# Four heads' first decay sums by TensorE, slot tables three passes ahead, a first network layer 44 steps ahead

## The chip, the core and the metric

The kernel runs on one core of one Trainium2 chip. The metric is the device time of one execution in microseconds, as the median of several runs. Three runs of the kernel before gave 884.05, 885.95 and 887.55 us, so its median is 885.95 us.

## The reference

Three stages follow each other, all in float32.

1. Attention with decay: batch 4, 8 heads, 576 positions, head size 64. The scores are `q·k/8`, plus `min(-(cum[i] - cum[j]), 0)`, where `cum` is the running sum of `max(s, 0)` along a head, under a causal mask; then softmax, then the product with `v`.
2. A mixture of experts over the 2304 rows of 512 numbers that attention leaves. Each row goes to the one expert (of 8) with the largest gate logit: `gate * relu(x @ w1[e]) @ w2[e]`, hidden size 1024.
3. A dense network: `h = x @ w_in` (2048 wide), `g = h * clip(h + 3, 0, 6) / 6`, `out = g @ w_out`.

The outputs are 2304 x 512 float32 numbers.

## The kernel before, in words

Products of float32 numbers are made of float16 halves: each operand is split into a high and a low half, and three products (high-high, high-low, low-high) stand for one. The splitting is done by ScalarE (high half) and VectorE or GpSimd (low half).

**Attention** runs over 20 units (a batch and a chunk of 128 rows, the last chunk 64), four pairs of heads to a unit. For a pair n, one turn of the main loop (from line 997 on) issues the transposes of pair n-1, the scores of pair n+1 (`S`, line 554), the addition of the decay sums with the row minimum on VectorE (`A`, line 567), the exponential on ScalarE (`E`, line 573), the split of the transposed weights (`CD`, lines 603 and 604), and the products with `v` of pair n-2 (`V`, line 637). `A` needs the decay sums of its head copied to all 128 partitions. These are made once: `s` is clipped and scaled (line 394), summed by one VectorE scan over 576 columns for the 32 rows of batch and head (line 395), put into an interleaved order of rows by ScalarE (lines 397 and 401), stored to DRAM as `cum_d` (line 403), and read back with one row copied to 128 partitions (`load_cum`, line 410) into the tile `cp`. For batch 0 the first 256 columns come first, in two loads: heads 0 and 1, then heads 2 to 7. Behind these, in the same queue of SyncE (SP), stand the loads of `v` for two row chunks, of `k` and `q` of the next 256 rows, and the five loads of the gate weights.

**The experts** run as 10 passes of 224, 224, 128, 128, 360, 336, 320, 296, 288 and 272 rows (numbers 0 to 9). The row numbers of a pass are a small table, `slots`, which SP loads from DRAM (`load_slots`, line 197). With it GpSimd gathers the rows (`gather`, line 204, up to three blocks of 128 rows by 2 KB), and SP transposes them by DMA into the tile `xsT` (`turn`, line 215). There are two buffers of `xsT`, one for even passes and one for odd ones. In pass p the rows of pass p+2 are gathered. Before the change the slots of pass p+2 are loaded in pass p too, just ahead of that gather (lines 1198 to 1201), for p from 3 on; those of passes 2 to 4 are loaded during pass 0. In pass p from 4 on, the weights of pass p+1 come in eight loads `wf` of 512 KB (line 239) through five staging buffers, and two or three pieces of `w_in` (`wd`, line 1049) through the same five; ScalarE and VectorE split them (lines 254 and 257, and 1037 to 1060). The first product of a pass is line 1109 (`ph`), whose result is turned into halves on ScalarE and VectorE (`hT`, lines 1113 and 1114); the second product is line 1221 (`py`).

**The network** has 9 chunks of 256 rows and 8 steps to a chunk, 72 steps in all. A first-layer step (`hidden_step`) is 24 matmuls (line 1247) into one PSUM bank; the bank is then clipped by ScalarE and VectorE (lines 1254 and 1255) and stored to DRAM (`t_d`). A second-layer step (`out_products`, line 1330) is 21 matmuls, three into each of seven banks in the order 6, 5, 4, 1, 0, 2, 3; what it needs is fetched back from `t_d` (`fetch`, lines 1307 to 1309) and combined (`sum_step`, lines 1318 to 1320, 1258 and 1259). The first `AHEAD` hidden steps use the seven banks in turn (step modulo 7); later ones use bank 7 alone. AHEAD is 40, so 41 hidden steps run before the first second-layer step, and after that one hidden step is made for two second-layer steps. During the first 41 steps, after every fifth, `convert` splits one of eight pieces of `w_out`, some 8 us of VectorE work each; it is tied behind the newest clip on VectorE.

**What sets the order.** Each engine works through its own queue in order, and so does SP with its DMA issues. The order in a queue is set when the program is built: the framework walks the instructions in the order of the program text, with modelled durations, and puts on each engine what is ready by that model. `issue_after` adds a fixed order on one engine. `at_slot(n, f)` calls f at the end of turn n of the attention loop.

Of the kernel before, what the change touches and what calls it, by code (L numbers as in the profile page):

```python
# [8 lines left out]
F32 = mybir.dt.float32  # L9
# [3 lines left out]
AF = mybir.ActivationFunctionType  # L13
ALU = mybir.AluOpType
# [21 lines left out]
def kernel(  # L36
# [16 lines left out]
    nc = tc.nc  # L53
    B, H, S, D = q.shape
# [10 lines left out]
    SC = 8.0  # L65
# [28 lines left out]
    idf = cst.tile([128, 128], F32, name="idf")  # L94
# [7 lines left out]
        out=upper, in_=upper, pattern=[[1, 128]], base=-1, channel_multiplier=-1,  # L102
# [47 lines left out]
    PF = 2 * NS  # L150
    rank_of = lambda p: NE - NS + p - NS if p < PF else p - PF
    NPASS = len(passes)
# [42 lines left out]
    def load_slots(p):  # L195
        n = (passes[p] + 127) // 128
        nc.sync.dma_start(slots[:, p, :n], rows_of(p, 128 * n).rearrange("(x q) o -> q x o", q=128))
# [24 lines left out]
    stage, mark = {}, {}  # L222
    rt = ctx.enter_context(tc.tile_pool(name="rt", bufs=2))
    psT = ctx.enter_context(tc.tile_pool(name="psT", bufs=3, space=PSUM))
# [79 lines left out]
    with ExitStack() as at:  # L304
        ac = at.enter_context(tc.tile_pool(name="ac", bufs=1))
        a2 = at.enter_context(tc.tile_pool(name="a2", bufs=2))
# [5 lines left out]
        kTs, cums, loaded, qTs, both = {}, {}, {}, {}, {}  # L312
# [34 lines left out]
        BH = B * H  # L347
        s_sb = a2.tile([BH, S], F32, tag="ne", name="s_sb")
# [20 lines left out]
        for o in (0, 64):  # L369
# [4 lines left out]
            for r in range(2):  # L374
                nc.gpsimd.affine_select(
                    out=mk[rows, r], in_=mk[rows, r], pattern=[[-1, 64]], base=0, channel_multiplier=1,
# [13 lines left out]
        zero = a2.tile([BH, S], F32, tag="ne", name="zero")  # L390
        nc.vector.memset(zero, 0.0)
        run = a2.tile([BH, S], F32, tag="pp", name="run")
        cum_sb = a2.tile([BH, S], F32, tag="pp", name="cum_sb")
        nc.vector.tensor_scalar(out=s_sb, in0=s_sb, scalar1=0.0, scalar2=SC, op0=ALU.max, op1=ALU.mult)
        nc.vector.tensor_tensor_scan(out=run, data0=s_sb, data1=zero, initial=0.0, op0=ALU.add, op1=ALU.add)
        nf = S // 128 * 128
        nc.scalar.activation(
            cum_sb[:, :nf].rearrange("h (j r p) -> h j p r", r=2, p=64),
# [6 lines left out]
        def load_cum(b, hs, a=0, z=S):  # L405

            if b not in cums:
                cums[b] = a2.tile([128, H, S], F32, tag="cp", name="cp")
            rows = cum_d.rearrange("(b h o) t -> b o h t", b=B, o=1)[b, :, hs, a:z]
            return nc.sync.dma_start(cums[b][:, hs, a:z], rows.partition_broadcast(128)[:, 0])  # L410

        def fold_cum(b, p):

# [437 lines left out]
        def at_slot(n, f):  # L851
            todo.setdefault(n, []).append(f)
# [21 lines left out]
        def then(f, *args):  # L874
            with tc.issue_after(last[0]):
                last[0] = f(*args).ins

        some, rest = slice(0, 2), slice(2, H)
        then(load_cum, 0, some, 0, 256)
        then(load_cum, 0, rest, 0, 256)  # L880
        then(load_v, 0, 0)
        then(load, 0, 1)
        then(load_v, 0, 1)
# [3 lines left out]
        then(load_v, 0, 2)  # L887
        then(load_v, 0, 3)
        then(load, 0, 2)
        for x, fs in enumerate(prep(0, 0, fast=True)):  # L890
            for f in fs:
                f() if x < 2 else at_slot(x - 3, f)
# [173 lines left out]
    HO = KO // 2  # L1066
# [60 lines left out]
    with ExitStack() as ex_:  # L1127
# [6 lines left out]
        jobs, pend = [], []  # L1134
        DOUBLES = {4: 3, 5: 3, 6: 3, 7: 2, 8: 2, 9: 3}
        for p, rows in enumerate(passes):
# [5 lines left out]
            if fresh:  # L1142
# [3 lines left out]
                jobs = new + jobs  # L1146
# [33 lines left out]
            for f in range(KF):  # L1180
# [10 lines left out]
                if p and f % 2 == 1:  # L1191

                    a, z = (min(sum(passes[:x]), NT) for x in (p, p + 1))
# [1 line left out]
                        with after("act"):  # L1195
                            nc.gpsimd.memset(x2T[:, f // 2::KD, a:z], 0.0)
                feed(f)
            if p >= PF - 1 and p + 2 < NPASS:
                load_slots(p + 2)
            if p and p + 2 < NPASS:  # L1200
                got = gather(p + 2)
                if p != NS:
# [13 lines left out]
            for d in range(KD):  # L1216
                py = pb.tile([128, 512], F32, tag="p", name="py")
                cols = slice(128 * d, 128 * d + 128)
                for f in range(KF):
                    for x, (i_, j_) in enumerate(((0, 0), (0, 1), (1, 0))):  # L1220
                        nc.tensor.matmul(  # L1221
                            py[:, :rows], wt2[:, j_, f, cols], hT[i_][:, f, :rows],
                            start=(f == 0 and x == 0), stop=(f == KF - 1 and x == 2),
# [43 lines left out]
    with ExitStack() as mx_:  # L1267
# [15 lines left out]
        jobs = [pair_piece(c, lambda c=c: w_sums[c]) for c in range(HO)]  # L1283
        pend = []
        TC = 256
        NSTEP = NT // TC * HO
        AHEAD = NSTEP - (NSTEP - HO) // 2
        t_d = dram.tile([NSTEP, 128, 512], F32, name="t_d")
        banks = [psT.tile([128, 512], F32, tag="T", name="bank") for x in range(3)]
        banks += [pb.tile([128, 512], F32, tag="p", name="bank") for x in range(5)]  # L1290
# [1 line left out]
        def hidden_step(s):  # L1292
            c, f = divmod(s, HO)
            x2 = x2T[:, :, TC * c:TC * c + TC]
            ph = banks[s % 7 if s < AHEAD else 7]
            for x, f_ in enumerate((f, f + HO)):
# [5 lines left out]
        def fetch(s):  # L1302


            if s < NSTEP:
                t = t_d[s].rearrange("p (a n) -> p a n", n=128)
                nc.sync.dma_start(back[s % 4][:, 0:2], t[:, 1:3])
                nc.sync.dma_start(back[s % 4][:, 2:4], t[:, 0::3])
                nc.sync.dma_start(back[s % 4][:, 4], t[:, 0])

        def sum_step(s):


            if s >= NSTEP:
                return
            vtt = nc.vector.tensor_tensor
            t, hi, lo = back[s % 4], sets[:, s % 4, 0], sets[:, s % 4, 1]
            vtt(out=t[:, 5:7], in0=t[:, 0:2], in1=t[:, 2:4], op=ALU.subtract)
            vtt(out=t[:, 7:9], in0=t[:, 0:2], in1=t[:, 3:5], op=ALU.add)
            vtt(out=t[:, 9], in0=t[:, 2], in1=t[:, 3], op=ALU.add)  # L1320
            halves_of(hi, lo, t[:, 3:10])
# [42 lines left out]
        def convert():  # L1364
            while jobs and len(pend) < 2:
                pend.append(jobs.pop(0)())
            if pend:
                with tc.issue_after(mark["clip"]):
                    pend.pop(0)()

        done = 0
        for l in range(NSTEP - 4):
            upto = min(NSTEP, AHEAD + l // 2 + 1)
            while done < upto:
                hidden_step(done)
                done += 1
                if done == 6:
                    nc.sync.dma_start(orows, row_d[:NT].rearrange("(c p) o -> p c o", p=128)[:, :, 2])
                if l == 0 and done % 5 == 1:
                    convert()  # L1380
                if done in (28, 30, 32, 34):
                    fetch((done - 28) // 2)
                if done in (37, 39):
                    sum_step((done - 37) // 2)
            fetch(l + 4)
            sum_step(l + 2)
            out_products(l)
            if l % HO == HO - 1:
                out_rows(l // HO)
# [8 lines left out]
    with ExitStack() as fb:  # L1398
# [5 lines left out]
        stop = nc.values_load(nblk, min_val=0, max_val=NT // 128)  # L1404
        with tc.For_i(0, stop, 1):
# [5 lines left out]
                out=t8, in0=iota8[:, None, 0].to_broadcast(of_all), in1=expert[:, :, None].to_broadcast(of_all), op=ALU.is_equal  # L1411
            )
            V.tensor_tensor(out=t8, in0=t8, in1=limit[:, None].to_broadcast(of_all), op=ALU.mult)
            rest, mine = f1.tile([128, NU], F32, name="rest"), f1.tile([128, NU], F32, name="mine")
# [6 lines left out]
            for x, m in enumerate((ones, upper)):  # L1421
# [3 lines left out]
                out=mine[:, 1:], data0=pn[:, 0, :NU - 1], data1=mine[:, 1:], initial=0.0, op0=ALU.add, op1=ALU.add  # L1425
# [13 lines left out]
            for u in range(NU):  # L1439
                n = R[units[u][1]]  # L1440
                nc.gpsimd.indirect_dma_start(
                    out=again_d[:, :], out_offset=Offset(ap=to[:n, u:u + 1], axis=0),
# [6 lines left out]
                out=xw, out_offset=None, in_=x_d[:, :], in_offset=Offset(ap=at[:, 0:1], axis=0)  # L1449
# [8 lines left out]
                out=sel, in0=iota8[:, 0], scalar1=ge[:, 3:4], scalar2=ge[:, 1:2],  # L1458
                op0=ALU.is_equal, op1=ALU.mult,
# [16 lines left out]
            for f in range(KO):  # L1476
# [11 lines left out]
                out=out[:, :], out_offset=Offset(ap=at[:, 2:3], axis=0), in_=o, in_offset=None,  # L1488
# [32 lines left out]
```

## Time and profile before

| | us |
|---|---|
| median of three runs | 885.95 |
| the profiled execution | 887.8 |
| its span in the profile | 886.1 |
| TensorE (PE) busy | 801.7 |
| VectorE (DVE) busy | 623.7 |
| ScalarE (ACT) busy | 461.8 |
| GpSimd (POOL) busy | 295.0 |

The profiled execution took 887.8 us, of which 886.1 us lie in the span that the trace covers. Attention fills the span up to about 290 us, the expert passes run from about 276 to 510 us, and the network from there to 874 us. In the rows, "L567" is line 567 of the kernel; a group reads "output<-inputs"; what stands in square brackets is the idle time of that engine just before, and what ended it. SPq is the DMA-issuing queue of SyncE. A matmul's duration includes its way through the array, so in a stream of matmuls the count in a stretch tells more than the durations.

### The profile page before, as it was taken

The numbers are of one execution on the slowest core, as the hardware profiler recorded it, in microseconds if no ns is written. First come the engines' busy times: TensorE is split into PE (matmuls) and PEld (weight loads), VectorE is DVE, ScalarE is ACT, GpSimd is POOL, SyncE is SP. The second block draws the span as 40 slices with busy tenths as digits, with TensorE's granted clock in tenths as the row PEclk, the third lists the DMA queues.
The fourth block names the chain that finished last, engine by engine and source line by source line (L and its number), as shares of the span: only waits on it lengthen the run. The fifth ranks groups of instructions, "written<-read, shape, count | busy, mean of one in ns | idle before, by whom it ended". The sixth has DMA issues, their size and how long they took to land. (4 is left out here: it accounts for less than half of the span.)

```text
span 886.1 us, 21854 instructions
## 1 busy us (share of the span) xinstructions
PE 801.7 (90%) x8332; PEld 661.9 (75%) x8332; DVE 623.7 (70%) x1545; ACT 461.8 (52%) x853; POOL 295.0 (33%) x397
## 2 busy tenths in 40 slices
PE   5898888779778989899998999999899999999993
PEld 3677666666558987566776888888788888888883
DVE  4787876766576653877787679878677677767770
ACT  3787776777854342665555444554334433343440
POOL 2585856689862222132430200000022022211222
PEclk9999999998789999999999999999999999999997
DMA  7966345333425486987879346544344444444430
GB/s 175 269 145 191 86 101 167 59 106 100 144 56 141 126 216 181 284 297 226 238 235 331 107 141 203 213 164 150 126 150 148 127 155 151 151 132 151 153 101 27
DMA packets 154327, 142.30 MB, mean 161 GB/s; under 512 B 68710, under 2 KB 122214, under 8 KB 153446
## 3 DMA queue, kind: packets, MB, share of 16 engines
q1 hardware_dynamic: 150422, 130.76, 49.9%
q0 software_dynamic: 3792, 10.06, 3.7%
q8 instruction: 67, 1.10, 0.5%
q14 instruction: 46, 0.38, 0.2%
HBM read 106.97 MB, written 28.54 MB: 153 GB/s over the span
## 5 line engine op out<-in xcount | busy, mean ns | idle before, releaser
L1247 PE MATMUL bank<-x2T,wi 128*128 128x256 f16 x1728 | 194.2, 273 | 0.6 <-POOL x2T L1229 0.5
L1247 PEld LDWEIGHTS <-wi 128*128 128x128 f16 x1728 | 169.1, 98 | 20.5 <-issue 1.0
L1330 PE MATMUL bank<-wo,sets 128*128 128x256 f16 x1512 | 172.7, 274 | 4.9 <-DVE cl L1255 4.0
L1330 PEld LDWEIGHTS <-sets 128*128 128x128 f16 x1512 | 148.5, 98 | 23.8 <-issue 4.4
L1221 PE MATMUL py<-hT,t 128*128 128x224 f16 (+7 forms) x960 | 111.0, 276 | 8.1 <-DVE hT L1114 6.7
L1258 ACT ACTIVATE sets<-back 128x896 f16<-128x896 f32 x72 | 68.2, 950 | 94.1 <-PE bank L1330 77.1
L1109 PE MATMUL ph<-xsT,t 128*128 128x224 f16 (+7 forms) x960 | 109.9, 276 | 7.3 <-DVE hT L1114 7.3
L1221 PEld LDWEIGHTS <-t 128*128 128x128 f16 x960 | 86.7, 99 | 31.2 <-issue 10.9
L1341 POOL TENSOR_TENSOR u<-sa 128x256 f32<-128x256 f32 x9 | 9.5, 1054 | 301.1 <-ACT sa L1340 301.1
L1109 PEld LDWEIGHTS <-t 128*128 128x128 f16 x960 | 86.2, 99 | 28.3 <-issue 8.0
L1259 DVE SCALAR_TENSOR_TENSOR sets<-back,sets 128x896 f16<-128x896 f32 x72 | 80.2, 1119 | 32.7 <-ACT sets L1258 32.6
L604 DVE SCALAR_TENSOR_TENSOR lo<-pt,hi 128x256 f16<-128x256 f32 (+3 forms) x144 | 72.7, 519 | 30.8 <-ACT hi L603 30.5
L257 DVE SCALAR_TENSOR_TENSOR t<-wf,t 128x1024 f16<-128x1024 f32 x53 | 64.5, 1221 | 36.6 <-ACT t L254 36.4
L582 PE MATMUL pt<-idf,pp 128*128 128x128 f32 (+1 forms) x400 | 77.1, 307 | 9.4 <-DVE den L649 3.6
L603 ACT ACTIVATE hi<-pt 128x256 f16<-128x256 f32 (+3 forms) x144 | 63.9, 461 | 41.4 <-PE pt L582 33.4
L254 ACT ACTIVATE t<-wf 128x1024 f16<-128x1024 f32 x53 | 55.6, 1055 | 45.0 <-DMA wf<-in_moe_w_dram 41.3
L573 ACT ACTIVATE pp<-ne,nm 128x128 f32<-128x128 f32 (+4 forms) x144 | 76.8, 580 | 4.3 <-DVE nm L567 4.1
L637 PE MATMUL o<-v,hi 128*128 128x65 f16 (+2 forms) x960 | 63.6, 203 | 14.6 <-ACT hi L603 7.8
L567 DVE CUSTOM_DVE_ANT_0 ne<-sp,cp 128x128 f32<-128x128 f32 (+4 forms) x144 | 61.1, 456 | 19.3 <-ACT pp L573 9.9
L637 PEld LDWEIGHTS <-hi 128*128 128x128 f16 (+2 forms) x960 | 49.0, 107 | 26.7 <-ACT hi L603 11.3
L582 PEld LDWEIGHTS pt<-idf,pp 128*128 128x128 f32 (+1 forms) x400 | 46.7, 151 | 19.2 <-remote 3.5
L637 PE MATMUL o<-v,lo 128*128 128x65 f16 (+2 forms) x480 | 54.2, 202 | 1.7 <-DVE lo L604 1.7
(202 smaller groups left out, 1231.5 us busy)
## 6 DMA issues: line engine op xcount, KB each, us to landing
wf<-in_moe_w_dram SPq DMA_DIRECT2D x64, 512.0 KB
back<-t_d SPq DMA_DIRECT2D x144, 128.0 KB
wd<-in_moe_w_in_dram SPq DMA_DIRECT2D x16, 512.0 KB
wd<-in_moe_w_out_dram SPq DMA_DIRECT2D x16, 512.0 KB
cp<-cum_d SPq DMA_DIRECT2D x6, 1152.0 KB
t_d<-cl SPq DMA_DIRECT2D x24, 256.0 KB
t_d<-sets SPq DMA_DIRECT2D x24, 256.0 KB
t_d<-wo SPq DMA_DIRECT2D x24, 256.0 KB
```

Of the source, the lines that this page charges most:

```text
L257: stt(out=lo, in0=fv, scalar=sc, in1=hi, op0=ALU.mult, op1=ALU.subtract)
L573: mark["act"] = nc.scalar.activation(self.view(self.pp, e), self.view(self.ne, e), AF.Exp, bias=self.nm[:, e:e + 1], scale=-1.0).ins
L582: nc.tensor.transpose(self.pt[g][:m, x, :], src, idf)
L603: nc.scalar.activation(hi, pt, AF.Copy, scale=SP)
L604: stt(out=lo, in0=pt, scalar=SP, in1=hi, op0=ALU.mult, op1=ALU.subtract)
L637: mark["pe"] = nc.tensor.matmul(dst, a, x, start=first, stop=last).ins
L1109: mark["pe"] = nc.tensor.matmul(ph[:, :n], wt[c][:, a, cols], xT[:, KD * b_ + c, :n], start=(c == 0 and x == 0), stop=(c == KD - 1 and x = ...
L1221: nc.tensor.matmul(py[:, :rows], wt2[:, j_, f, cols], hT[i_][:, f, :rows], start=(f == 0 and x == 0), stop=(f == KF - 1 and x == 2),)
L1247: m = nc.tensor.matmul(dst, wi[:, a, kk, fs], x2[:, KD * b_ + kk], start=(kk == 0 and x == 0), stop=(kk == KD - 1 and x == 2),)
L1258: nc.scalar.activation(hi, t, AF.Copy, scale=SG)
L1259: stt(out=lo, in0=t, scalar=SG, in1=hi, op0=ALU.mult, op1=ALU.subtract)
L1330: m = nc.tensor.matmul(banks[k_][:, :HM], sets[:, s % 4, a, k_], w_sums[f][:, b_, k_], start=(f == 0 and x == 0), stop=(f == HO - 1 and x ...
```

## The change

Four edits are made.

- The clip of `s` and the scan are each cut in two: columns 0 to 127 first, then 128 to 575, with the second scan starting from the last column of the first.
- `first_cum` makes the decay sums of heads 0 to 3 for the first 128 columns on TensorE: for each head a float32 product of a column of the identity (copied to 128 columns) with the 32 x 128 running sums, into one PSUM bank of the pool that the transposes use, and one ScalarE copy of 128 x 512 into `cp`. It is called at slot -1. The two loads from `cum_d` change: heads 4 to 7 of columns 0 to 255 first, then heads 0 to 3 of columns 128 to 255.
- The slots of pass p+3 are loaded in pass p, for p from 2 to 6.
- AHEAD becomes 44, so that 45 hidden steps run before the first second-layer step, and then 7 hidden steps are made for 16 second-layer steps. The first fetches and sums keep their distance to AHEAD. The first piece of `w_out` is no longer tied behind the newest clip.

```diff
-        nc.vector.tensor_scalar(out=s_sb, in0=s_sb, scalar1=0.0, scalar2=SC, op0=ALU.max, op1=ALU.mult)
-        nc.vector.tensor_tensor_scan(out=run, data0=s_sb, data1=zero, initial=0.0, op0=ALU.add, op1=ALU.add)
+        for a, z in ((0, 128), (128, S)):
+            nc.vector.tensor_scalar(out=s_sb[:, a:z], in0=s_sb[:, a:z], scalar1=0.0, scalar2=SC, op0=ALU.max, op1=ALU.mult)
+            nc.vector.tensor_tensor_scan(
+                out=run[:, a:z], data0=s_sb[:, a:z], data1=zero[:, a:z], initial=run[:, a - 1:a] if a else 0.0,
+                op0=ALU.add, op1=ALU.add,
+            )
...
+        FIRST = 4
+        def first_cum():
+            if 0 not in cums:
+                cums[0] = a2.tile([128, H, S], F32, tag="cp", name="cp")
+            pc = psT.tile([128, FIRST, 128], F32, tag="T", name="pf")
+            for h in range(FIRST):
+                nc.tensor.matmul(
+                    pc[:, h], idf[:BH, h:h + 1].to_broadcast([BH, 128]),
+                    run[:, :128].rearrange("h (p r) -> h r p", r=2),
+                    start=True, stop=True,
+                )
+            nc.scalar.activation(cums[0][:, :FIRST, :128], pc, AF.Copy)
...
-        some, rest = slice(0, 2), slice(2, H)
-        then(load_cum, 0, some, 0, 256)
-        then(load_cum, 0, rest, 0, 256)
+        then(load_cum, 0, slice(FIRST, H), 0, 256)
+        then(load_cum, 0, slice(0, FIRST), 128, 256)
...
+        at_slot(-1, first_cum)
...
-            if p >= PF - 1 and p + 2 < NPASS:
-                load_slots(p + 2)
+            if p >= PF - 2 and p + 3 < NPASS:
+                load_slots(p + 3)
...
-        AHEAD = NSTEP - (NSTEP - HO) // 2
+        AHEAD = NSTEP - (NSTEP - HO) // 16 * 7
...
-                with tc.issue_after(mark["clip"]):
+                with tc.issue_after(mark["clip"]) if len(jobs) < HO - 2 else ExitStack():
                     pend.pop(0)()
...
-            upto = min(NSTEP, AHEAD + l // 2 + 1)
-            while done < upto:
+            upto = AHEAD + l // 16 * 7 + len([x for x in (0, 2, 4, 6, 8, 11, 14) if x <= l % 16])
+            while done < min(upto, NSTEP):
...
-                if done in (28, 30, 32, 34):
-                    fetch((done - 28) // 2)
-                if done in (37, 39):
-                    sum_step((done - 37) // 2)
+                if done in range(AHEAD - 12, AHEAD - 4, 2):
+                    fetch((done + 12 - AHEAD) // 2)
+                if done in (AHEAD - 3, AHEAD - 1):
+                    sum_step((done + 3 - AHEAD) // 2)
```

## Rows read from the trace of the kernel before

**Rows 1.** Page, part 1: busy us, share of the span, instructions of each engine.

```profile
PE 801.7 (90%) x8332; PEld 661.9 (75%) x8332; DVE 623.7 (70%) x1545; ACT 461.8 (52%) x853; POOL 295.0 (33%) x397
```

**Rows 2.** Windows of 50 us: busy us (instructions) by engine, granted clock, DMA share, GB/s.

```profile
0.00:50.00 50.00, 37.11 (x372) 25.83 (x373) 32.12 (x141) 29.36 (x66) 23.02 (x47) 0.97 0.85 209
...
350.00:400.00 50.00, 45.64 (x295) 29.22 (x293) 37.72 (x56) 29.41 (x44) 12.87 (x14) 0.97 0.88 289
```

**Rows 3.** Timeline from the start: start, us, engine, line, what, count [idle before].

```profile
5.07 1.33 DVE L395 TENSOR_TENSOR_SCAN run<-s_sb,zero 32x576 f32<-32x576 f32 x1
...
5.40 0.60 ACT L477 ACTIVATE kT<-pk 128x512 f16<-128x512 f32 x1 [3.29 <-PE pk L469]
...
6.57 1.46 PE L469 MATMUL pk<-idf,k 128*128 128x128 f32 x4
...
9.28 0.88 SPq L410 DMA_DIRECT2D cp<-cum_d  x2
...
9.48 0.26 PE L554 MATMUL sp<-dg,sel 64*128 64x64 bf16 x2
...
13.99 0.29 DVE L567 CUSTOM_DVE_ANT_0 ne<-sp,cp 128x128 f32<-128x128 f32 x1 [4.60 <-DMA cp<-cum_d]
...
16.69 0.29 DVE L567 CUSTOM_DVE_ANT_0 ne<-sp,cp 128x128 f32<-128x128 f32 x1 [1.59 <-DMA cp<-cum_d]
```

**Rows 4.** Timelines of ACT, POOL and DVE, 22 to 27 us.

```profile
22.54 0.64 ACT L493 ACTIVATE v<-v 128x512 f16<-128x512 f32 x1 [3.48 <-DMA v<-in_v_dram]
...
24.48 0.22 POOL L424 TENSOR_SCALAR wg<-wgf 128x32 f16<-128x32 f32 x1 [1.53 <-DMA wgf<-in_moe_w_gate_dram]
...
26.16 0.41 DVE L567 CUSTOM_DVE_ANT_0 ne<-sp,cp 128x256 f32<-128x256 f32 x1
```

**Rows 5.** Waits of PE, 340 to 490 us: us in total, times, longest.

```profile
PE py L1221 <- DVE hT L1114: 6.3, 9, 1.3
PE ph L1109 <- DVE hT L1114: 3.8, 2, 2.4
```

**Rows 6.** Waits of ACT, 345 to 500 us.

```profile
ACT t L254 <- DMA wf<-in_moe_w_dram: 33.7, 22, 7.1
```

**Rows 7.** Timeline of the SP queue in pass 5 (376 to 405 us) and after.

```profile
389.99 0.38 SPq L197 DMA_DIRECT2D slots<-tok_d  x1
390.48 2.90 SPq L1049 DMA_DIRECT2D wd<-in_moe_w_in_dram  x3
400.92 3.99 SPq L215 DMA_TRANSPOSE xsT<-xg  x3
...
408.10 6.25 SPq L239 DMA_DIRECT2D wf<-in_moe_w_dram  x6
```

**Rows 8.** Timeline of POOL in passes 1 and 5: gathers.

```profile
303.14 0.98 POOL L204 DMA_INDIRECT xg<-x_d,slots  x1 [0.30 <-issue]
...
395.51 0.98 POOL L204 DMA_INDIRECT xg<-x_d,slots  x1 [12.13 <-issue]
```

**Rows 9.** Waits of the SP queue, whole span.

```profile
SPq L215 <- DMA xg<-x_d,slots: 46.0, 11, 8.6
```

**Rows 10.** Window of 15 us in pass 5, columns as in rows 2.

```profile
385.00:400.00 15.00, 13.88 (x97) 9.20 (x95) 13.82 (x21) 10.63 (x16) 3.24 (x3) 1.00 0.94 343
```

**Rows 11.** Windows of 10 us around the first second-layer step.

```profile
620.00:630.00 10.00, 6.47 (x45) 5.09 (x44) 5.41 (x10) 4.34 (x7) 0.00 (x0) 0.83 0.35 125
630.00:640.00 10.00, 10.00 (x94) 8.96 (x92) 7.09 (x14) 3.27 (x4) 0.00 (x0) 1.00 0.38 112
```

**Rows 12.** Timeline, 596 to 624 us: ACT, DVE and PE.

```profile
602.28 0.67 ACT L1037 ACTIVATE m<-wd 128x512 f32<-128x512 f32 x1 [4.37 <-DMA wd<-in_moe_w_out_dram]
...
613.50 0.76 DVE L1038 TENSOR_SCALAR m<-m 128x512 f32<-128x512 f32 x2
...
622.80 0.68 DVE L1255 SCALAR_TENSOR_TENSOR cl<-cl,bank 128x512 f32<-128x512 f32 x1
...
623.53 5.32 PE L1330 MATMUL bank<-wo,sets 128*128 128x256 f16 x32 [3.97 <-DVE cl L1255]
```

## The prediction

> **What bounds the kernel now.** I read the busy shares first: PE 90%, DVE 70% [rows 1]. That is an average over stages with different limits, so next come the windows. From 630 us on PE is busy 10.00 of 10 us with 94 matmuls in that time [rows 11]; nothing that the change does can make that stretch shorter, since the 72 x 24 first-layer and 72 x 21 second-layer matmuls stay. Where PE is not full, the change may act: in the first 50 us (37.11 busy), and in the expert passes (45.64 of 50) [rows 2], and in the ten microseconds in which the second layer begins, with 45 matmuls in place of 94 [rows 11]. In each of the three I then looked, in the timeline and the waits, for what ends the idle time last.
>
> **The head, removed.** DVE stands 4.60 us until the sums of heads 0 and 1 have come back from DRAM, adds them at 13.99, and stands 1.59 us more for heads 2 to 7 at 16.69 [rows 3]. **Added** are the float32 products and a copy. The scan is 1.33 us for 576 columns; 128 are 0.30 us by the ratio, an estimate. Four float32 products of 128 columns are not in the trace; the nearest row is four float32 transposes of the same width, 1.46 us with their waits for loads, and the bounds are 0.3 us (hidden in PE's waits) and, at twice that row, 2.9 us. The copy of 128x512 is 0.60 us by the first kT copy [rows 3]. So 5.07 + 0.30 + 1.46 + 0.60 = 7.4 us, before the scores of pair 0, whose last products start at 9.48 [rows 3]. PE and ACT are both busy with the first transposes then, so I put the addition at about 9.8: 4.2 us earlier. The split clip and scan add two short DVE instructions, which reach the store of `cum_d` some 0.2 us later.
>
> **What is late next in the head.** Heads 4 to 7 are needed by pair 2. Between 13.99 and 16.69 the old second load brought 6 heads x 256 x 4 B x 128 partitions, 0.79 MB: 0.29 MB/us. The new first load has 0.52 MB in place of 0.26, so it lands about 0.9 us after 13.99, the second (0.26 MB) at 15.8, or 16.7 if rows of half the length cost double. Then the old limits stand: ACT stood 3.48 us for `v` until 22.54, POOL waited for the gate weights until 24.48, and DVE came to pair 5 only at 26.16 [rows 4]. These loads stand behind in the same SP queue and come earlier only by what is not loaded any more, 1.05 - 0.79 = 0.26 MB, 0.9 us. So the gain is 4.2 us if pairs that run earlier fill the wait for `v`, 0.9 if they don't, and -1 if the added PE and ACT work (2.1 us) stands half on the path. I take 1.5, nearer to the row of the `v` wait than to the sum's.
>
> **The slots.** In pass 5 the slots are issued at 389.99, behind the weight loads. POOL, idle 12.13 us, gathers at 395.51; the trace shows nothing that it waited for, but the slots are what it reads [rows 7, 8]. SP then stands until the gathered rows have landed: its three wd issues end at 393.38, the transposes start at 400.92, and only behind them, at 408.10, the next pass's weights [rows 7]. Over the span that stand of SP is 46.0 us in 11 waits, up to 8.6 [rows 9]. The cost is paid further on: ACT waits 33.7 us for `wf` [rows 6], the halves `hT` come late on DVE, and PE waits 6.3 + 3.8 = 10.1 us for them [rows 5]. With the slots a pass earlier the gather can go as soon as POOL is free. Where slots are there in time the trace shows this: in pass 1, whose gathers use slots from pass 0, one starts at 303.14, 0.30 us after the one before [rows 8]. Four gathers of 3 blocks (in passes 4 to 7) and the one in pass 3 move so. Moved with them are their transposes (3 SP issues each), which are now limited by the `xsT` buffer: it comes free when PE ends the first product of the same pass. Moved past them are the wd loads of the same pass, which may stand up to 4.0 us (the transposes' issue, [rows 7]) behind. The slot load itself stays where it was in SP's queue, 0.38 us, with one register load; pass 2 gets one more, pass 7 one less. The gain is at most 10.1 us. At nothing I can cost it if SP's stand only changes its cause; the loss is the slower rival below. The stand of 393.38 to 400.92, 7.5 us, is as long as the longest wait of ACT for `wf`, 7.1 [rows 6, 7], but the five staging buffers come free one by one, so I don't give the whole: I take 6.0.
>
> A rule of the Trainium skill speaks against this part. The row: in 385 to 400 us, where the gathers would go, the DMA share is 0.94 at 343 GB/s [rows 10]. The rule ("DMA: Bandwidth & Descriptors", section on queues, rings and completion order): each of the shared DMA engines takes turns between the queues that have work, so the gather takes its share from the weight loads. By the row alone the gain is 6.0; by the rule it is less, as the fourth rival has it.
>
> **The second layer's start.** PE waits 3.97 us at 623.53 for the clip at 622.80, and the granted clock of that window is 0.83; the loss is (94 - 45)/94 x 10 = 5.2 us [rows 11, 12]. Before that, ACT stood 4.37 us at 602.28 for a piece of `w_out`, with the clips behind it, and the last of eight conversions began on DVE at 613.50 [rows 12]. From there to the awaited clip's end, 623.48, it is 10.0 us for a conversion and four clips (of steps 36 to 39). PE runs a step in 24/94 x 10 = 2.55 us. With 45 steps ahead the last conversion still comes after step 35, but eight clips follow before the banks must be free: 10.0 + 4 x 0.68 = 12.7 us of DVE against 8 x 2.55 = 20.4 us of PE. The slack of 7.7 us is above the wait of 3.97. The last of these banks, 1 (step 43), comes fourth in the order, with a step and nine matmuls (3.5 us) ahead of it, against 1.4 us for a clip on two engines, twice 0.68. So the wait goes; I take 5.0 of 5.2, between 0 and 5.2. The untied first conversion, four more stores before the first fetch and the rate of 7 in 16 I cost at nothing: they lie beside a full PE, and if this cover fails they show as waits of line 1330, not more than the 5.2 that is there now.
>
> **The sum.** 1.5 + 6.0 + 5.0 = 12.5 us. The profiled execution took 887.8: 875.3. It lies 1.85 above the median of the runs, 885.95, so for a median I say 873.5.
>
> **Rivals.**
> - Everything that waits now goes: 4.2 + 10.1 + 5.2 = 19.5, 866.5 as a median. For it: the waits have one cause each. Against: the `v` load of the head, and DVE is busy 13.82 of 15 us in pass 5 [rows 10]. Chance 0.14.
> - SP's stand changes its cause: transposes wait for the `xsT` buffer where they waited for the gather, weights come no earlier, part two is 0: 879.5. For it: only two buffers. Against: in pass 5 the stand lies after the first product's end. Chance 0.16.
> - The wait at the second layer stays, since ACT still stands for `w_out` pieces: gain 1 there, 877.5. For it: the 4.37 us. Against: the slack of 7.7. Chance 0.08.
> - The gather shares: 3 x 128 x 2 KB = 0.79 MB at 343 GB/s are 2.3 us by which weights come later, in four passes 9.2, so part two is 6.0 - 9.2 = -3.2: 882.7. Against: the same bytes were moved in the same pass before, only some 10 us later. This is the Trainium skill's rule from above. Chance 0.05.
> - Slower: the transposes are put in SP's queue ahead of the last two wf and the three wd loads, and SP stands there until the first product has ended. In pass 5 that is near 390, and 4.0 us of issue follow, so loads that started from 386 start at 394: 8 us late, of which PE pays half, in four passes 16 us. Then 887.8 - 1.5 - 5.0 + 16 is 897.3, as a median 895.5. It decides from 6.5/4 = 1.6 us more of PE waits in each pass. For it: the order in SP's queue is set by modelled times. Against: the loads are ahead in the program's text. Chance 0.07.
>
> The forecast itself has 0.50, with 869 to 878 as its own range. A measurement of this kernel can tell about 0.5%, 4.4 us: faster means below 881.5. Faster holds the forecast, the first and third rival and two thirds of the second, 0.50 + 0.14 + 0.08 + 0.11 = 0.83; same 0.05 + 0.05 = 0.10; slower 0.07. The range of 864 to 883 leaves out the slower rival and some 0.05 on either side.
>
> **What would show it.** Head: the first L567 near 10 us in place of 13.99; the fifth pair's stays near 24 to 26. Slots: gathers in passes 4 to 7 with no 12 us of POOL idle before them; the wait of L215 on `xg` well under 46.0; the wf loads of pass 6 issued before 404; PE's wait on hT under 5 us. Second layer: no wait of L1330 over 1 us at its start, and a clock of 1.00 there. The prediction is wrong if PE's waits on hT stay at 10 us although the gathers are early, or if a new wait of L1330 on a clip stands where the old one was.

## The result, and the profile after

The changed kernel takes 876.72 us (median of 4 runs, 874.39 to 878.73) against 885.15 us for the kernel before (4 runs): a ratio of 0.990 (95% interval 0.987 to 0.994). The forecast was 873.5 us, with a range of 864 to 883. The profiled execution took 878.73 us; its line of busy times (engine, us, share of the span, instructions) answers to [rows 1]:

```profile
span 877.0 us, 21872 instructions
...
PE 796.4 (91%) x8340; PEld 659.6 (75%) x8340; DVE 623.7 (71%) x1547; ACT 461.7 (53%) x854; POOL 292.8 (33%) x397
```

These shares hardly tell the two kernels apart. What does is a cut of the span at the first row of each stage in PE's timeline. The rows below are the first expert product, the first product of the network's first layer, the first of its second layer, and PE's last row; first of the kernel after, then of the one before.

```profile
273.10 2.46 PE L1130 MATMUL ph<-xsT,t 128*128 128x224 f16 x24
...
498.85 1.51 PE L1268 MATMUL bank<-x2T,wi 128*128 128x256 f16 x10
...
624.60 5.01 PE L1351 MATMUL bank<-wo,sets 128*128 128x256 f16 x42 [0.79 <-DVE wo L1276]
...
855.36 8.14 PE L1351 MATMUL bank<-wo,sets 128*128 128x256 f16 x73 [0.73 <-DVE sets L1280]
```

```profile
276.00 2.46 PE L1109 MATMUL ph<-xsT,t 128*128 128x224 f16 x24
...
509.92 1.51 PE L1247 MATMUL bank<-x2T,wi 128*128 128x256 f16 x10
...
618.30 1.25 PE L1330 MATMUL bank<-wo,sets 128*128 128x256 f16 x10
...
863.84 8.14 PE L1330 MATMUL bank<-wo,sets 128*128 128x256 f16 x73 [0.50 <-DVE sets L1259]
```

So attention ends 2.9 us earlier; the experts take 225.75 us in place of 233.92 (8.2 less); the network, from its first product to PE's end, 364.65 in place of 362.06 (2.6 more). 2.9 + 8.2 - 2.6 = 8.5 of the 9.1 us by which the span is shorter. Two parts won and one lost.

**Head.** Timelines of PE, ACT and DVE of the kernel after:

```profile
5.58 2.07 PE L426 MATMUL pf<-run,idf 32*128 32x128 f32 x8
...
7.77 0.57 ACT L431 ACTIVATE cp<-pf 128x512 f32<-128x512 f32 x1
...
11.21 0.29 DVE L588 CUSTOM_DVE_ANT_0 ne<-sp,cp 128x128 f32<-128x128 f32 x1 [0.52 <-PE sp L575]
...
17.62 0.64 ACT L514 ACTIVATE v<-v 128x512 f16<-128x512 f32 x1 [3.10 <-DMA v<-in_v_dram]
...
18.57 0.42 DVE L588 CUSTOM_DVE_ANT_0 ne<-sp,cp 128x256 f32<-128x256 f32 x1 [3.33 <-ACT pp L594]
...
24.32 0.19 DVE L360 SCALAR_TENSOR_TENSOR wg<-wgf,wg 128x32 f16<-128x32 f32 x1 [4.97 <-POOL wg L445]
...
26.51 0.41 DVE L588 CUSTOM_DVE_ANT_0 ne<-sp,cp 128x256 f32<-128x256 f32 x1
```

The first addition (L588) comes at 11.21, 2.8 us before the old one [rows 3], and waits for its scores, no longer for a load. But ACT now stands 3.10 us for `v` with an exponential queued behind it, DVE stands behind that exponential and then for the gate weights, and pair 5 (the sixth, counted from 0), which came at 26.16 [rows 4], comes at 26.51. Two pairs on, the new kernel is behind: pair 7 starts at 33.62, before the change at 30.73 (DVE's timeline):

```profile
30.73 0.42 DVE L567 CUSTOM_DVE_ANT_0 ne<-sp,cp 128x256 f32<-128x256 f32 x1
```

**Slots.** Waits of PE, 340 to 490 us; of ACT, 345 to 500 us; of SP, whole span; then SP's timeline in pass 5, and a gather in POOL's:

```profile
PE ph L1130 <- DVE hT L1135: 2.5, 1, 2.5
PE py L1242 <- ACT hT L1134: 1.5, 2, 1.2
PE py L1242 <- DVE hT L1135: 0.4, 1, 0.4
...
ACT t L254 <- DMA wf<-in_moe_w_dram: 29.0, 21, 8.3
...
SPq L215 <- DMA xg<-x_d,slots: 23.0, 10, 5.9
```

```profile
378.95 1.78 SPq L239 DMA_DIRECT2D wf<-in_moe_w_dram  x2
...
382.05 3.29 SPq L1070 DMA_DIRECT2D wd<-in_moe_w_in_dram  x3
386.88 7.29 SPq L215 DMA_TRANSPOSE xsT<-xg  x3
395.90 0.64 SPq L1233 DMA_DIRECT2D row_d<-tok_d  x1
397.42 3.30 SPq L239 DMA_DIRECT2D wf<-in_moe_w_dram  x5
...
405.68 0.98 POOL L204 DMA_INDIRECT xg<-x_d,slots  x1 [0.39 <-issue]
```

PE's waits for VectorE's half of `hT` fall from 10.1 us [rows 5] to 2.9 (for ScalarE's half they are 0.9 and 1.5), SP's wait for gathered rows from 46.0 [rows 9] to 23.0, ACT's for `wf` only from 33.7 [rows 6] to 29.0. From the start of the wd loads to that of the next pass's wf loads it is 15.4 us in place of 17.6 [rows 7]. POOL's idle 12.13 us before a gather [rows 8] is gone.

**Network.** The wait of 3.97 us at the second layer's start [rows 12] is 0.79 (the row at 624.60), and the window of 620 to 630 us holds 77 matmuls at a clock of 1.00, in place of 45 at 0.83 [rows 11]:

```profile
620.00:630.00 10.00, 8.72 (x77) 7.38 (x76) 4.72 (x9) 3.94 (x6) 0.00 (x0) 1.00 0.44 160
```

In its place the first layer waits nine times for a bank, which the kernel before did not. PE's timeline (three of the nine rows), then DVE's and ACT's where it begins:

```profile
555.87 10.64 PE L1268 MATMUL bank<-x2T,wi 128*128 128x256 f16 x96 [0.82 <-DVE wo L1276]
...
577.80 8.14 PE L1268 MATMUL bank<-x2T,wi 128*128 128x256 f16 x72 [0.47 <-DVE sets L1276]
...
607.82 4.43 PE L1268 MATMUL bank<-x2T,wi 128*128 128x256 f16 x38 [0.63 <-DVE wo L1276]
...
515.34 0.42 DVE L1339 TENSOR_TENSOR back<-back 128x256 f32<-128x256 f32 x1 [5.75 <-DMA back<-t_d]
...
553.52 0.42 DVE L1110 SCALAR_TENSOR_TENSOR wo<-m,wo 128x256 f16<-128x256 f32 x1 [5.33 <-ACT wo L1109]
...
549.20 0.68 ACT L1058 ACTIVATE m<-wd 128x512 f32<-128x512 f32 x1 [3.26 <-DMA wd<-in_moe_w_out_dram]
...
552.51 0.67 ACT L1058 ACTIVATE m<-wd 128x512 f32<-128x512 f32 x1 [2.63 <-DMA wd<-in_moe_w_out_dram]
```

A step takes PE 2.62 us here, and not the 2.55 of the prediction: before the change 974 matmuls of this layer take 106.49 us without a wait, and a step is 24 of them. First that row, then the one of the kernel after that leads up to the first wait:

```profile
511.98 106.49 PE L1247 MATMUL bank<-x2T,wi 128*128 128x256 f16 x974 [0.55 <-POOL x2T L1229]
```

```profile
500.95 54.09 PE L1268 MATMUL bank<-x2T,wi 128*128 128x256 f16 x494 [0.59 <-POOL x2T L1250]
```

A bank is written again seven steps later, so a clip has to end within 6 x 2.62 = 15.7 us of the end of its own step; later than that, PE stands. Call the time from the step's end to the clip's end its lag. In the kernel before the largest lag of the first 41 clips is 12.4 us. Here the 15th step ends at 539.2 (10 matmuls before 500.95, 350 of 0.109 us from there); its clip starts at 555.13, takes 0.68 and so lags 16.7, and the 22nd step, which needs that bank, starts at 555.87 after the first of the nine waits. From there PE stands itself, and with its waits in between the lag grows to 18.8 at the 33rd clip. DVE had lost 5.75 us to an early sum and 5.33 to a conversion, and clips stood behind both.

### The profile page after: what moved, and what is told of

It is laid out like the page before. It is cut to its first block, busy times and chain, and to the rows that moved or that the text cites. A ratio compares the mean times of both kernels' runs of the same rounds, so it can differ in the third digit from the quotient of the medians.

```text
span 877.0 us, 21872 instructions
## 1 busy us (share of the span) xinstructions
PE 796.4 (91%) x8340; PEld 659.6 (75%) x8340; DVE 623.7 (71%) x1547; ACT 461.7 (53%) x854; POOL 292.8 (33%) x397
## 5 line engine op out<-in xcount | busy, mean ns | idle before, releaser
L1351 PE MATMUL bank<-wo,sets 128*128 128x256 f16 x1512 | 170.3, 273 | 2.2 <-DVE wo L1276 0.8
L1242 PE MATMUL py<-hT,t 128*128 128x224 f16 (+7 forms) x960 | 108.2, 273 | 2.1 <-ACT hT L1134 1.5
L603 PE MATMUL pt<-idf,pp 128*128 128x128 f32 (+1 forms) x400 | 74.6, 300 | 7.2 <-DVE kT L499 2.0
L624 ACT ACTIVATE hi<-pt 128x256 f16<-128x256 f32 (+3 forms) x144 | 64.2, 462 | 29.2 <-PE pt L603 28.8
L588 DVE CUSTOM_DVE_ANT_0 ne<-sp,cp 128x128 f32<-128x128 f32 (+4 forms) x144 | 61.1, 455 | 15.6 <-ACT pp L594 10.8
L1250 POOL TENSOR_TENSOR x2T<-y,x2T 128x360 f32 (+5 forms) x24 | 21.2, 888 | 113.5 <-ACT x2T L1249 81.9
L1339 DVE TENSOR_TENSOR back<-back 128x256 f32<-128x256 f32 x72 | 34.3, 477 | 34.4 <-DMA back<-t_d 32.3
```

What stands on the lines that cost most here:

```text
L603: nc.tensor.transpose(self.pt[g][:m, x, :], src, idf)
L624: nc.scalar.activation(hi, pt, AF.Copy, scale=SP)
L1242: nc.tensor.matmul(py[:, :rows], wt2[:, j_, f, cols], hT[i_][:, f, :rows], start=(f == 0 and x == 0), stop=(f == KF - 1 and x == 2),)
L1351: m = nc.tensor.matmul(banks[k_][:, :HM], sets[:, s % 4, a, k_], w_sums[f][:, b_, k_], start=(f == 0 and x == 0), stop=(f == HO - 1 and x ...
```

## The experiments

Each kernel was timed against the kernel before in five rounds; those of one group (1 to 4, 5 to 8, 9 to 12) shared a chip. The ratios are those on record and not the quotients of the medians that are quoted below. The stages come from the same rows as above, of one profiled execution each.

```
kernel              ratio   95% interval    1st expert  experts  network  wait at 2nd layer
before                -                      276.00     233.92   362.06   4.0
after               0.990   0.987 to 0.994   273.10     225.75   364.65   0.8
1 e1_head           0.9995  0.996 to 1.003   270.27     231.71   364.64   6.0
2 e2_slots          0.994   0.990 to 0.998   272.51     225.20   360.28   2.5
3 e3_net            1.001   0.997 to 1.004   276.45     231.21   360.90   0.8
4 e4_head_slots     0.988   0.983 to 0.994   272.29     223.02   357.99   1.9
5 e5_whole          0.989   0.985 to 0.994   279.04     225.92   364.01   0.8
6 e6_tied           0.980   0.975 to 0.986   280.19     224.07   358.43   0.2
7 e7_abs_late       0.986   0.981 to 0.991   281.40     225.82   357.49   0
8 e8_abs_late_..    0.986   0.981 to 0.991   278.59     224.56   364.13   5.5
9 e9_turn_late      0.992   0.989 to 0.995   274.92     221.28   360.56   2.9
10 e10_head_gate    1.004   1.001 to 1.007   282.32     234.14   363.61   5.4
11 e11_tied_abs_..  0.982   0.978 to 0.986   275.35     223.70   356.59   0
12 e12_all          0.989   0.984 to 0.995   284.55     223.84   356.65   0
```

The end of attention differs by 4 us between kernels with the same attention on one chip (2 and 3) and by up to 9 between chips (4 and 7), so that column is read only within a group and beyond that. Experts and network repeat within 1 us between two traces of the whole change on two chips (225.75 and 225.92; 364.65 and 364.01). Between kernels whose expert part is the same they differ by 3 us: 231.21 to 234.14 in the four with the old slots (before, 1, 3 and 10), 223.02 to 225.92 in the nine with the new ones.

**1 to 4: one part at a time, and the first two together.** Edits: the diff's own parts (scan, first sums and loads; the slots line; the network's lines).

```diff
+        at_slot(-1, first_cum)                       # 1 and 4, with the split scan and loads
-            if p >= PF - 1 and p + 2 < NPASS:
+            if p >= PF - 2 and p + 3 < NPASS:        # 2 and 4
-        AHEAD = NSTEP - (NSTEP - HO) // 2
+        AHEAD = NSTEP - (NSTEP - HO) // 16 * 7       # 3, with the untied first conversion
```

> The head edit alone (first decay sums on TensorE, split scan, the two loads). Theory A, read from the two traces: the first addition moves from 13.99 to 11.2 us, but pair 5 stays at 26 us behind the loads of v and of the gate weights, so the head gives nothing; the 2.9 us by which the expert stage starts earlier (first ph matmul 276.0 before, 273.1 after) come from a changed order later in attention. Then this kernel starts the experts at about 273 and takes 882 us. Rival: the 2.9 us need another part of the change as well (or are chance); then the experts start at 276 and the time is 885.

> The slot edit alone (slots of pass p+3 loaded in pass p). Theory A: the expert stage, from the first ph matmul to the first network matmul, falls from 233.9 to about 226 us, the gathers of passes 5 to 7 start 6 to 14 us earlier, PE's waits for hT between passes 4 and 8 fall from 10 to 4 us or less; the time is 877 us. Rival: half of the 8.2 us that the expert stage lost comes from the different start of the stage; then 881 us.

> The network edit alone (AHEAD 44, 7 hidden steps in 16, first conversion untied). Theory A: VectorE is the engine that is late in the hidden steps, so the wait of 3.97 us at the first second-layer step becomes many waits of line-1268 matmuls for free banks; the network grows by about 2 us, the time is 887. Rival, the prediction: the wait goes and nothing takes its place; 880 us.

> Head and slots together, the network as before. Theory A (the parts add): 885.2 - 2.9 - 8.2 = 874.0 us, so 2 to 3 us below the whole change. Rival, the prediction's: the network edit gains, so that without it the time is 880 or more.

Of the single parts only the slots are faster (877.16 us beside 884.21). The head alone is 882.93, the network alone 883.42: neither can be told from nothing. Head and slots together, 870.27, have a ratio of 0.988, as good as the whole change's; their network stage, in the old order, is 6.7 us shorter than in the whole change. Alone, in 3, the new order waits 1.1 us for banks and its stage is 1.2 us shorter than before, where I had expected it about 2 us longer; on top of the other two it lost.

**5 to 8: what makes the clips late.** 5 is the whole change again. 6 takes back one line of it. 7 and 8 put each conversion on ACT, too, behind the latest clip in the program (7 on the whole change, 8 on head and slots with the old network order).

```diff
-                with tc.issue_after(mark["clip"]) if len(jobs) < HO - 2 else ExitStack():
+                with tc.issue_after(mark["clip"]):                                            # 6
+                with after("clip", "relu") if len(jobs) < HO - 2 else ExitStack():            # 7
+        mark["relu"] = nc.scalar.activation(t, ph, AF.Relu, bias=three, scale=SH).ins         # 7, 8
```

> The whole change again, beside its own variants on one chip. What head and slots gave without the new network order was a ratio of 0.988; the whole gave 0.990. Theory A (the new network order gives back at its front what it gains at its start of the second layer): 0.990 to 0.992, 2 to 4 us behind head and slots with the old network, the stage from the first L1268 product to PE's end at 363 to 366 us. Rival (the network edit is a gain that was hidden by noise): 0.985, the stage at 358.

> The whole change, but the first conversion is tied behind the clips again, as before the change. Theory A (ACT's first step of a conversion, L1058, stands 4 to 5 us for a piece of w_out with clips queued behind it, whichever conversion comes first): within 2 us of the whole change, L1268's waits for banks still 4 us or more. Rival C (the untied conversion pushes all clips back): 4 us faster than the whole, L1268's waits under 2 us.

> The whole change, and each conversion is tied on ACT, too, behind the latest clip in the text, so that L1058 no longer stands ahead of clips. Theory A: ACT's wait of L1058 for w_out pieces falls from 32 us to under 15, L1268's waits for banks from 5.3 to under 2, the stage from the first L1268 product to PE's end from 364.6 to 358 to 360, the time 870 to 872 (4 to 7 us under the whole change). Rival B (DVE simply has too much to do there: 8 conversions of 10 us, 44 clips of 0.68, the first sums 13 us, together 123 us in 125): within 2 us of the whole change, the bank waits stay at 4 us or more.

> Head and slots as in the change, the old network order (40 steps ahead), and the conversions tied on ACT as well. Theory A: L1058's waits fall as well, but with 40 steps the wait at the second layer's start (1.9 us in one trace, 4.0 in another) is set by the last conversion on DVE, so 0 to 3 us under head and slots alone: 868 to 871, and not below the whole change with the same tie by more than 1 us. Rival B: no change to head and slots alone, 870 to 872, and 4 us or more below the whole change with the tie.

Both mends take the bank waits of the first layer away: 876.87 (6) and 881.24 us (7) beside 884.63 for the whole change on the same chip, and network stages of 358.43 and 357.49 beside 364.01. (For 7 the stage shows it; the single times of 7 and 5, 878 to 887 and 882 to 888, overlap.) In 6 ACT waits as long for pieces of `w_out` as in the whole change, so that stand alone is not the cause, and theory A as I had put it falls. The untied conversion (rival C) alone isn't either: in 7 it stays untied, the stand is gone and the bank waits too. The two add up to the lag, and taking away either is enough. Run 3 has both as well, without the other two edits, and waits only 1.1 us; what makes them weigh more in the whole change was not parted. Rival B, that DVE has simply too much to do, falls with both mends. Waits of ACT in the kernel after and in 6 (504 to 630 us), of PE in 6, and DVE's rows of 6 that answer to 555.13 and 553.52:

```profile
ACT m L1058 <- DMA wd<-in_moe_w_out_dram: 32.3, 12, 5.0
```

```profile
ACT m L1058 <- DMA wd<-in_moe_w_out_dram: 30.2, 12, 4.5
...
PE bank L1268 <- DVE wo L1276: 1.2, 1, 1.2
...
549.85 0.69 DVE L1276 SCALAR_TENSOR_TENSOR wo<-wo,bank 128x512 f32<-128x512 f32 x1
...
554.24 0.42 DVE L1110 SCALAR_TENSOR_TENSOR wo<-m,wo 128x256 f16<-128x256 f32 x1 [2.76 <-ACT wo L1109]
```

The 15th clip (549.85) lags 6.0 us in 6 in place of 16.7. The largest lag of the first layer's clips is 15.1 in 6, 14.6 in 7 and 13.2 in 11, all under 15.7, and PE waits for no clip in the first 45 steps of these three (the 1.2 us of 6 come behind them, at 629.73). In 3 it is 16.2, and there PE waits 0.28 us. In 8, with the same tie and the old order, the wait at the second layer's start is 5.5 us (1.9 in 4, without the tie and on another chip), which theory A had not foreseen.

**9: the slots as late as before, the transposes later.** On the kernel before: SP's transposes for pass p+2 stand in pass p+1 in the program, between its weight loads.

```diff
+                if f == 5 and p > NS and p + 1 < NPASS:
+                    xs[p + 1] = turn(p + 1, got)
...
-                if p != NS:
+                if p < NS:
                     xs[p + 2] = turn(p + 2, got)
...
-            if p == NS:
-                xs[p + 2] = turn(p + 2, got)
```

> The kernel before with slots and gathers as late as they were; only the transposes of the gathered rows stand one pass later in the program, between the next pass's weight loads, so that SP never stands for a gather. Theory S (what the slots edit gains is SP's stand in front of the weight loads, not the early gather itself): L215's wait on xg falls from 46 us to under 10, the expert stage (first hidden product to first network product) from 233.9 to 225 to 228, as with the slots edit alone (225.2), ratio 0.993 to 0.996. Rival D (the early gather matters): the stage stays at 231 to 234, ratio 0.998 to 1.002.

880.4 beside 889.7 us, and the shortest expert stage of all, 221.28: the slots need not be loaded a pass earlier. Yet L215 waits 41.9 us on `xg`, not under 10 as I had expected, and most of that still stands ahead of the weight loads: in 340 to 480 us these waits are 28.8 us, 29.5 before the change and 3.6 after. So theory S had the stage right and the reason wrong; SP's stand for the gathered rows is not by itself what costs. What 9 changes is what follows a stand: one transpose in place of three is left ahead of the first wf loads, and the other two come between them. In time the gathers come earlier, too, though the program has them where they were, since SP reaches the slots sooner: the last group of gathers starts 62.4 us ahead of the network (433.81 to 496.20), in place of 57.3 before and 65.7 after. How much of the gain is due to the order in SP's queue and how much to the earlier gather this run doesn't part. Waits of ACT (345 to 500 us), of SP, and SP's timeline:

```profile
ACT t L254 <- DMA wf<-in_moe_w_dram: 21.6, 23, 3.6
...
SPq L215 <- DMA xg<-x_d,slots: 41.9, 8, 8.5
```

```profile
376.24 2.46 SPq L1049 DMA_DIRECT2D wd<-in_moe_w_in_dram  x3
384.92 1.30 SPq L215 DMA_TRANSPOSE xsT<-xg  x1
386.52 0.63 SPq L1214 DMA_DIRECT2D row_d<-tok_d  x1
387.44 2.62 SPq L239 DMA_DIRECT2D wf<-in_moe_w_dram  x4
390.11 1.64 SPq L215 DMA_TRANSPOSE xsT<-xg  x1
...
392.58 1.34 SPq L215 DMA_TRANSPOSE xsT<-xg  x1
```

SP stands from 378.70, the end of the wd issues, to 384.92. From the wd loads to the wf loads it is 11.2 us, in place of 17.6 before and 15.4 after.

**10: four gate loads behind the head's other loads**, on the head edit alone.

```diff
-        for to, src in gate_in:
+        for to, src in gate_in[:1]:
             then(nc.sync.dma_start, to, src)
...
         then(load, 0, 2)
+        for to, src in gate_in[1:]:
+            then(nc.sync.dma_start, to, src)
```

> The head edit alone, and four of the five small gate loads, whose issues take SP 3 us at 19 to 22 us, are issued after the head's other loads; their half of the weights is split at slot 14. Theory F (the head's early start is given back to the loads behind it in SP's queue): the loads of sums, v and k behind them come 2 to 3 us earlier, pair 8 goes from 33.5 to 31, and the time to 2 to 3 us under before: ratio 0.9965 to 0.998. Rival G (it is given back to v and k that stand ahead of the gate loads): pair 8 stays at 33 to 34, ratio 0.999 to 1.000, as the head edit alone had it (0.9995).

Pair 7 counted from 0, the eighth ("pair 8" above), comes 3.2 us earlier, as theory F said. First its row with the head edit alone, then with this one (DVE's timelines):

```profile
33.53 0.42 DVE L588 CUSTOM_DVE_ANT_0 ne<-sp,cp 128x256 f32<-128x256 f32 x1
```

```profile
30.36 0.42 DVE L588 CUSTOM_DVE_ANT_0 ne<-sp,cp 128x256 f32<-128x256 f32 x1
```

That is no more than where the kernel before already had it, 30.73. And the kernel is slower, 893.31 beside 889.7 us (ratio 1.004, 1.001 to 1.007). Theory F is right that these loads hold that pair back, and wrong that the time would come back at the end.

**11 and 12: both mends; and both with the gate loads moved.** The edits of 6 and 7 together, then with that of 10.

> The whole change with both mends of the network order: the first conversion tied behind the clips again, and all conversions tied on ACT as well. Theory A with C (both keep the clips less than 15 us behind PE, which is what seven banks allow): stage from the first network product to PE's end 357 to 358.5, ratio 0.980 to 0.985, no more than either alone gave (0.980 and 0.986), since PE then waits for no bank. Rival (the two add up): stage 354 to 355.5, ratio under 0.979.

> As the run with both mends, and the gate loads behind the head's other loads. By theory F 2 to 3 us under that run, by rival G the same within 1 us.

11 takes 871.94 us beside 889.7, a ratio of 0.982; its network stage is within 2 us of either mend alone, so they don't add up. This kernel is faster than the one before. Its interval (0.978 to 0.986) lies below that of the whole change in the first result (0.987 to 0.994) and just overlaps that of run 5 (0.985 to 0.994), both on other chips. 6 has about the same ratio; which is better isn't settled.

12 loses 7 us to 11 on the same chip, all of it in attention (first expert product at 284.55, in 11 at 275.35). Its eighth pair comes 3.1 us earlier than in 11, its 17th only 0.7, and the last addition 7.3 us later. There ACT stands 5.9 us for routing, which it does not in 11; in 10 it is 5.6, but in 1, without moved loads, 3.3 too (waits of ACT in 12, 250 to 285 us):

```profile
ACT ex L751 <- POOL eq L747: 5.9, 1, 5.9
```

Why moved loads of the head change the order at attention's end was not followed further.

## Why the prediction was right or wrong, by its steps

**Head: 1.5 us forecast, none of its own measured** (ratio 0.9995, 0.996 to 1.003). The addition was put at 9.8 and came at 11.21: the four products make eight records of 2.07 us (within the bounds 0.3 to 2.9; I took 1.46), and they stand ahead of the last transposes of `q` and `k`, so pair 0's scores end at 11.3. "What is late next" was named rightly, `v` and the gate weights, but I let a third of the gain through and nothing came through: pair 5 came at 26.51, close to the 24 to 26 at which I had said it would stay, and pair 7 came 2.9 us later than before. Run 10 takes that loss back, and no time is found again at the end.

**Slots: 6.0 us forecast, about 8 measured.** The ratio of 0.994 (0.990 to 0.998) is 5.0 us of 885, with 1.6 to 8.5; the expert stage is 8.2 to 8.7 us shorter in traces 2 and after than in the one before. Over all traces but that of run 9 it is 232.7 us on average with the old slots (four) and 224.7 with the new (nine), 8.1 less, and at least 5.3. The steps came as described: gather early, PE's waits on `hT` 10.1 to 2.9, `wf` issued at 397.42, before the 404 that I had set. But run 9 doesn't bear out the step in the middle, that SP's stand for the gathered rows is what costs: it stands as long as before, and the stage is the shortest. What both kernels share is that the wf loads come sooner behind the wd loads (15.4 and 11.2 us in place of 17.6) and that the gathers come earlier. What the slower rival started from did not come about: in pass 5 the transposes (386.88) stand behind the last two wf (378.95) and the wd loads (382.05). The fourth rival, that the gather shares with the weight loads (the Trainium skill, "DMA: Bandwidth & Descriptors", section on queues, rings and completion order, has them take turns), would have made the stage 3.2 us longer; no run shows such a price.

**Network: 5.0 us forecast, 2.6 lost.** Here the prediction failed, in this step: "The untied first conversion, four more stores before the first fetch and the rate of 7 in 16 I cost at nothing: they lie beside a full PE, and if this cover fails they show as waits of line 1330, not more than the 5.2 that is there now." The cover did fail; the waits came in the first layer, at the line that is 1268 after the change, not at the second layer's 1330, and cost 5.6 to 6.5 us (364.01 in run 5 against 358.43 and 357.49 with a mend). The slack of 7.7 us was worked out from the last conversion to the second layer's start alone. What decides is the lag of every clip before it, against the 15.7 us that seven banks allow. The kernel before had 12.4, so 3.3 us to spare; the untied conversion, together with ACT's stands for `w_out`, took more than that.

There was also less to win than the 5.2 us of [rows 11, 12], because the parts don't add. With the slots edit or run 9 the old order's wait is 2.5, 1.9 and 2.9 us, without it 4.0, 6.0 and 5.4 (run 8, with its tie, is an exception at 5.5; all are single traces). So the mended network order (356.59 to 358.43) is hardly shorter than the old order in run 4 (357.99). Why the slots edit shortens that wait was not tried.

**The sum** came within 3.2 us of the median because the network's miss (7.6 us) was partly made good by slots (2.2 more) and by an attention stage that ended 2.9 us earlier (1.4 more than the head's 1.5), which the runs can't assign to an edit. That the sum came so near is luck: one of its three terms had the wrong sign, and another gave nothing of its own. What was written down as the sign of a wrong prediction, a new wait of L1330 on a clip in place of the old one, is there in substance: the wait at the second layer's start is 0.79 us, under the 1 us that was set, but nine waits on clips stand in the first layer.

## What to carry to other kernels

Work that is urgent pays for everything ahead of it in an in-order queue, so look at what could stand behind it there as well as at making a late input early: run 9, which moves only transposes in SP's program, gained as much as the earlier slots, though the gathers came earlier with it. Work that is moved ahead "beside a full engine" has to be counted against the number of buffers: follow the consumer's lag through the whole stage, buffer by buffer, and not only at the point that was late. Time saved in front of a chain of loads is not worth more than the next load allows.

## What was not expected of the hardware

The four float32 products of 32 by 128 rows and 128 columns show as eight records, 2.07 us together, where four float32 transposes of that width take 1.46 [rows 3], and 1.06 at 8.28 in PE's timeline of the kernel after.

In the kernel after the granted clock falls to 0.57 in 14 to 16 us, after waits of PE of 1.12 us and less, and is 0.50 (the level of 1.2 GHz) from 16 to 30, with a wait of 2.98 us for `v` in it; before, it is 1.00 there. The rows don't bear that difference out. Two mask products of the scores (`mk`, 64x128) take 0.22 us in the kernel after where the clock is 1.00 and 0.31 where it is 0.50; in the kernel before they take 0.31 as well at 18.63, where the figure is 1.00, and 0.22 at 31.12. By its rows PE is as slow there before the change as after it, so the lower figure is no cost of the edit (the ends of matmuls are modelled). First two rows of after, then two of before:

```profile
10.92 0.22 PE L575 MATMUL sp<-mk,sel 64*128 64x128 bf16 x2
...
19.07 0.31 PE L575 MATMUL sp<-mk,sel 64*128 64x128 bf16 x2
```

```profile
18.63 0.31 PE L554 MATMUL sp<-mk,sel 64*128 64x128 bf16 x2
...
31.12 0.22 PE L554 MATMUL sp<-mk,sel 64*128 64x128 bf16 x2
```

At the second layer's start a longer wait goes with a loss greater than itself: over six traces of the old network order (before and runs 1, 2, 4, 9 and 10) the network stage grows from 357.99 us at a wait of 1.9 to 364.64 at 6.0, which is 1.6 us for each us waited. In the profile's windows of 10 us with a wait of 4.0 to 6.0 us the granted clock is 0.80 to 0.83; with 1.9 us it is 1.00. (With 2.5 and 2.9 us the lowest window is 0.83 and 0.90.) What else differs between these six was not parted from the wait.
